# TensorE's unread products in a clustered-attention and softplus-FFN kernel: counts from a rule against counts from a table

## The chip, the cores and the metric

The kernel runs on one core of a Trainium2 chip. The metric is the device time of one execution in microseconds (us); the time shown is the median of several runs, and a profiled execution gives the trace.

## The reference

Inputs are float32 q, k, v of shape (4, 8, 768, 64), centroids (8, 16, 64) and two FFN matrices, 512 x 2048 and 2048 x 512. Every query and key row is assigned to the nearest of 16 normalized centroids of its head; a query attends only to keys of its own cluster. The heads are then joined, and a two-layer network with softplus follows.

```
q_assign = np.argmax(np.einsum('bhsd,hcd->bhsc', q_n, c_n), axis=-1)
k_assign = np.argmax(np.einsum('bhsd,hcd->bhsc', k_n, c_n), axis=-1)
mask = q_assign[:, :, :, None] == k_assign[:, :, None, :]
scores = np.where(mask, scale * np.matmul(q, k.transpose(0, 1, 3, 2)), -1e9)
attn = np.exp(scores - np.max(scores, axis=-1, keepdims=True))
attn = attn / (np.sum(attn, axis=-1, keepdims=True) + 1e-09)
x = np.matmul(attn, v)                    # (B, H, S, D) -> (B*S, H*D)
h = x @ w_in
out = (np.maximum(h, 0.0) + np.log1p(np.exp(-np.abs(h)))) @ w_out
```

## The kernel before

The work is cut into tiles of 128 query rows of one head, 192 in all, taken in eight passes of three row blocks for each of the eight heads. For each tile `scores` (L1101, tile `s`) makes 128 x 768 scores, VectorE takes their negated maximum (L1117, `negm`), ScalarE the exponential (L1126, `p`), and `p` is split into two half-precision parts and transposed: in the first tiles by TensorE (L1143, `pT`), later by a transposing DMA (`pt<-phl`). `attend` (L1239, or L1243 and L1244, into the PSUM tile `mbank`) multiplies by V. Every pass ends in the FFN: `ffn1` (L1331 to L1333, tile `h`), softplus on VectorE, ScalarE and GpSimd, and `ffn2` (L1425 to L1427, tile `o`). The first keys and queries are transposed on TensorE (`turn`, L803, tiles `kT` and `qT`, copied out at L547), compared with the centroids (L822 and L823, tiles `sim_k`, `sim_q`) and masked by a chain of small VectorE operations (L835 to L846, L908); `clusters` counts the clusters in use (L927 on TensorE, L942 on VectorE, `al`).

The order of all instructions is written out: `SEQUENCE` is a list of the numbers of the chains of work, and `Order.run` issues the next operation of the chain that each entry names. `Order` keeps a modelled clock for each engine beside it. The order of entries is the order in the program, engine by engine.

Between these operations TensorE is given products that nobody reads: 128 columns of `ones`, cut to 120, times an identity (L521). `warm` decides on them, before each TensorE operation, from the modelled idle time ahead of it. Where `mbank` is not yet in use they go into its last 120 columns (`idle`), and else into a free one of the three banks of `ps_u` (tile `fill`):

```
gap = end - max(begin, ready)
if gap > (150 if begin < 30000 else WARM_FROM):
    out = idle if spot == 9 else ps_u.tile([P, 512], F32, tag=f"u{spot}", name="fill")[:, :WARM]
    for _ in range(int(gap * (0.95 if begin < 2500 else 0.75 if begin < 30000 else WARM_SHARE) / (100 if begin < 2500 else 52))):
        nc.tensor.matmul(out, eye, ones[:, :WARM], start=True, stop=True)
```

Of the kernel before, what the change touches and what calls it, by code (L numbers as in the profile page):

```python
# [9 lines left out]
F32 = mybir.dt.float32  # L10
# [27 lines left out]
FIRST = 3  # L38
PAIR = 425
WARM = 120  # L40
WARM_FROM = 600
WARM_SHARE = 0.65
FLIP = 180.0
SLACK = 0
BIAS = 500
# [60 lines left out]
]  # L106
SEQUENCE = [
# [166 lines left out]
class Order:  # L274
# [9 lines left out]
    def __init__(self):  # L284
        self.free = {"PE": 1800.0, "DVE": 2500.0, "ACT": 2000.0, "POOL": 2700.0, "SP": 1000.0}
        self.ev, self.blocked, self.active = {}, {}, {}
        self.dma = 0.0
        self.loads = 0
        self.shared = {"DVE": [], "POOL": []}
        self.rings = {}  # L290
        self.cur, self.seq = None, 0
        self.warm = None
        self.mb = [0.0, 0.0]
        self.ranks = iter(RANKS)
        self.mread = 0.0
        self.claims, self.line, self.given = 0, [], {}
        self.held = dict.fromkeys(CAPS, 0)
        self.idle = [("bank", i, 0) for i in range(3)]
        self.ev.update(dict.fromkeys(self.idle, 0.0))
# [104 lines left out]
        return t  # L404

    def run(self):
        for code in SEQUENCE:
            which, seq = divmod(code, 1000)
            ch = self.active.pop(seq)
            _, eng, ns, emit, opt = ch["op"]  # L410
            if isinstance(eng, tuple):
                eng, ns, emit = eng[which], ns[which], emit[which]
            start = self.start(ch, eng, ns)
            if eng == "PE" and self.warm:
                self.warm(self.free["PE"], start)
            self.free[eng] = start + ns - self.PIPE[eng]
            end = start + ns + self.LAT[eng]
            if "flip" in opt:
                self.dma = max(self.dma, start + 900) + opt["flip"]
                self.free[eng] = max(start + ns, self.dma - 1600)  # L420
                end = max(self.dma, self.free[eng]) + 650
            elif "load" in opt:
                self.dma = max(self.dma, start + 900) + opt["load"] + (self.loads == 2) * 1200
                self.loads += 1
                end = max(self.dma, start + ns) + 1350
            if "mb" in opt:
                self.mb[opt["mb"]] = max(self.mb[opt["mb"]], end)
            emit()
            ch["now"] = end
            self.pump(ch)  # L430
        assert not self.blocked and not self.active
# [3 lines left out]
def tile_cluster_attention__then__softplus_ffn(  # L435
# [10 lines left out]
    nc = tc.nc  # L446
# [4 lines left out]
    P = 128  # L451
# [13 lines left out]
            name=nc.get_next_instruction_name(),  # L465
# [10 lines left out]
    ps_u = ctx.enter_context(tc.tile_pool(name="ps_u", bufs=1, space=bass.MemoryType.PSUM))  # L476
# [6 lines left out]
    for c in range(NCL):  # L483
        nc.vector.memset(tab[:, :, c : c + 1], float(NCL - c))

    eye = cpool.tile([P, P], F16, name="eye")
    nc.gpsimd.memset(eye, 0.0)
    nc.gpsimd.affine_select(
        out=eye, in_=eye, compare_op=ALU.not_equal, fill=1.0, base=0, pattern=[[-1, P]], channel_multiplier=1
# [4 lines left out]
    ones = cpool.tile([P, P], F16, name="ones")  # L494
# [13 lines left out]
    od = Order()  # L508
# [2 lines left out]
    mbank = ps_m.tile([P, 512], F32, name="mbank")  # L511
    idle = mbank[:, 512 - WARM :]

    def warm(begin, end):

        ready, spot = min([(od.ev[b], b[1]) for b in od.idle] + [(od.mread, 9)])
        gap = end - max(begin, ready)
        if gap > (150 if begin < 30000 else WARM_FROM):
            out = idle if spot == 9 else ps_u.tile([P, 512], F32, tag=f"u{spot}", name="fill")[:, :WARM]
            for _ in range(int(gap * (0.95 if begin < 2500 else 0.75 if begin < 30000 else WARM_SHARE) / (100 if begin < 2500 else 52))):  # L520
                nc.tensor.matmul(out, eye, ones[:, :WARM], start=True, stop=True)  # L521

    od.warm = warm

# [687 lines left out]
    def attend(t: int):  # L1212
# [6 lines left out]
        if t:  # L1219
            yield wait("at", t - 1)  # L1220
        pt, ptk = pts.pop(t)
        od.mread = math.inf
        t0 = t - t % (2 * nt)
        if whole(t):
            if t == t0:
# [248 lines left out]
    first, begin = {}, []  # L1474
# [13 lines left out]
    for t in range(len(tiles)):  # L1488
        od.spawn(scores(t), t)
        od.spawn(attend(t), t + LAG)  # L1490
# [45 lines left out]
```

## Time and profile before

| what | value |
| --- | --- |
| median of 3 runs | 822.16 us (822.07 to 824.63) |
| profiled execution, its own time | 822.05 us |
| span of its trace | 820.3 us |
| TensorE (PE) busy | 804.5 us, 98% of the span |
| VectorE (DVE), ScalarE (ACT), GpSimd (POOL) busy | 656.3, 563.4 and 543.9 us |
| products at L521 | 269: 187 up to 28.2 us, 82 between 102.4 and 586.6 us |

The time of a run is the span and the little that lies around it. TensorE takes its instructions in order, so a product at L521 holds up whatever stands behind it if that is ready, and costs nothing if it is not. A matmul's row gives the time until its result is out, which reaches into the next one's; the distance between two starts is what one costs in a stream. "Idle before" stands in square brackets, with the work that ended it.

### The profile page before, as it was taken

Reading aid. Unit: us, or ns where it says so; the run is one execution under the profiler, and the core shown is the slowest. Engines: PE = TensorE matmul, PEld = TensorE weight load, DVE = VectorE, ACT = ScalarE, POOL = GpSimd, SP = SyncE. Lnnn points to the kernel's source line nnn. Section 1 sums busy time; section 2 is a strip of 40 time slices with the busy share of each in tenths; the row PEclk is TensorE's granted clock in tenths of the full one; section 3 lists DMA queues with packets and bytes.
Section 4 is the critical chain, followed back from the end, with each engine's and each line's share of the span. In section 5 each row is a group of like instructions: output and inputs, shape, how many; then the busy total and the mean of one; then the engine's idle time right before and its main releaser. Section 6 shows DMA issues by size and latency. Waiting matters only on the chain.

```text
span 820.3 us, 17681 instructions
## 1 busy us (share of the span) xinstructions
PE 804.5 (98%) x6914; PEld 514.2 (63%) x6914; DVE 656.3 (80%) x1124; ACT 563.4 (69%) x1084; POOL 543.9 (66%) x421
## 2 busy tenths in 40 slices
PE   8999999999999999999999999999999999999998
PEld 8888876555666666566666666565666565655554
DVE  7999999998898888888998878969877888743222
ACT  6998899987677767774866867576666656644441
POOL 5856486848877879876477777776876874523340
PEclk9999999999999999999999999999999999999999
DMA  9254999999999999999988988999888885730001
GB/s 334 97 164 142 219 204 237 209 203 212 180 180 193 187 206 182 219 187 173 183 178 172 166 197 180 197 182 196 159 161 151 152 161 110 130 59 13 26 1 40
DMA packets 386228, 134.16 MB, mean 164 GB/s; under 512 B 362464, under 2 KB 379104, under 8 KB 386144
## 3 DMA queue, kind: packets, MB, share of 16 engines
q1 hardware_dynamic: 386144, 133.03, 78.2%
q8 instruction: 54, 0.88, 0.4%
q14 instruction: 30, 0.25, 0.1%
HBM read 35.68 MB, written 6.29 MB: 51 GB/s over the span
## 4 chain that ended last, share of the span: by engine, by line
PE 75%; DMA 7%; DVE 6%; ACT 6%; POOL 3%; issue 3%; SPq 0%; DVEq 0%; ACTq 0%; POOLq 0%
PE s L1101 11%; PE o L1427 8%; PE o L1425 8%; PE o L1426 8%; PE h L1331 8%; PE h L1333 8%; PE h L1332 8%; PE mbank L1243 5%; DMA pt<-phl 4%; PE mbank L1244 3%; PE mbank L1239 2%; POOL phl L556 1%; ACT p L1126 1%; DVE negm L1117 1%; DMA rawk<-in_k_dram 1%
## 5 line engine op out<-in xcount | busy, mean ns | idle before, releaser
L1126 ACT ACTIVATE p<-s,negm 128x768 f32<-128x768 f32 x190 | 170.9, 900 | 77.5 <-DVE negm L1117 55.8
L1117 DVE TENSOR_REDUCE negm<-s 128x1 f32<-128x768 f32 x192 | 181.2, 949 | 25.4 <-PE s L1101 24.6
L556 POOL TENSOR_TENSOR phl<-p,phl 128x768 f16<-128x768 f32 x98 | 171.4, 1754 | 39.1 <-ACT phl L574 26.2
L1331 PE MATMUL h<-xT,wi 128*128 128x384 f16 x512 | 166.9, 326 | 0.6 <-DVE fg L1380 0.3
L1333 PE MATMUL h<-xT,wi 128*128 128x384 f16 x512 | 166.9, 326 | 0.0
L1332 PE MATMUL h<-xT,wi 128*128 128x384 f16 x512 | 166.9, 326 | 0.0
L1101 PE MATMUL s<-kt,qt 128*128 128x384 f16 x768 | 156.3, 326 | 4.6 <-ACT p L1126 2.4
L1425 PE MATMUL o<-wo,gh 128*128 128x512 f16 (+2 forms) x392 | 146.6, 375 | 0.6 <-DVE ot L1458 0.6
L1427 PE MATMUL o<-wo,gh 128*128 128x512 f16 (+2 forms) x392 | 146.5, 375 | 0.3 <-DVE gh L556 0.3
L1426 PE MATMUL o<-wo,gh 128*128 128x512 f16 (+2 forms) x392 | 146.5, 375 | 0.0
L1243 PE MATMUL mbank<-vb,pt 128*128 128x128 f16 x1008 | 107.6, 220 | 0.5 <-DMA pt<-phl 0.4
L556 POOL TENSOR_TENSOR gh<-fg,gh 128x768 f16<-128x768 f32 x47 | 80.2, 1707 | 36.4 <-ACT gh L574 17.5
L1244 PE MATMUL mbank<-vb,pt 128*128 128x64 f16 x1008 | 103.2, 193 | 0.0
L1101 PEld LDWEIGHTS <-qt 128*128 128x128 f16 x768 | 71.0, 98 | 48.8 <-issue 4.4
L1386 POOL TENSOR_TENSOR fg<-fg,fa 128x384 f32<-128x384 f32 x53 | 58.5, 1105 | 63.6 <-ACT fa L1378 61.9
L1243 PEld LDWEIGHTS <-pt 128*128 128x128 f16 x1008 | 89.6, 98 | 14.2 <-DMA pt<-phl 3.0
L1244 PEld LDWEIGHTS <-pt 128*128 128x128 f16 x1008 | 87.7, 98 | 10.9
L1362 ACT ACTIVATE fa<-h 128x384 f32<-128x384 f32 x84 | 41.0, 488 | 68.9 <-PE h L1333 51.4
L574 ACT CAST phl<-p 128x768 f16<-128x768 f32 x87 | 71.4, 827 | 17.4 <-DMA pt<-phl 14.4
L556 DVE TENSOR_TENSOR phl<-p,phl 128x768 f16<-128x768 f32 x64 | 71.0, 1113 | 4.2 <-POOL phl L574 2.4
L1377 ACT ACTIVATE fa<-fa 128x384 f32<-128x384 f32 x128 | 66.5, 522 | 9.6 <-DVE fa L1358 8.9
L1332 PEld LDWEIGHTS <-wi 128*128 128x128 f16 x512 | 50.1, 98 | 34.9 <-issue 1.8
(193 smaller groups left out, 1429.8 us busy)
## 6 DMA issues: line engine op xcount, KB each, us to landing
wo<-in_moe_w_in_dram SPq DMA_DIRECT2D x8, 1024.0 KB, 7.7
rawk<-in_k_dram SPq DMA_DIRECT2D x16, 384.0 KB, 3.9
rawq<-in_q_dram SPq DMA_DIRECT2D x16, 384.0 KB, 4.2
rawv<-in_v_dram SPq DMA_DIRECT2D x16, 384.0 KB, 4.0
wo<-in_moe_w_out_dram SPq DMA_DIRECT2D x6, 1024.0 KB, 5.7
out_dram<-ot SPq DMA_DIRECT2D x23, 256.0 KB, 2.6
pt<-phl SPq DMA_TRANSPOSE x82, 5.7
wo<-in_moe_w_out_dram SPq DMA_DIRECT2D x2, 512.0 KB, 4.0
```

The source lines that it names most:

```text
L556: [lambda e=e: e.tensor_tensor(dst, a, b, ALU.subtract) for e in (nc.gpsimd, nc.vector)],
L1101: nc.tensor.matmul(st[:, j, :SH], qt[:, s, i], kt[:, s, NT // 2 * j : NT // 2 * (j + 1)], start=(s == 0), stop=(s == 1),)
L1117: yield op("DVE", 950, lambda: nc.vector.tensor_reduce(negm, st[:, :, :SH], AX.XY, ALU.max, negate=True))
L1126: yield op("ACT", 980, lambda: nc.scalar.activation(ex, st[:, :, :SH], AF.Exp, bias=negm, accum_out=total))
L1243: nc.tensor.matmul(av, pt[:, 0, c], vb[:, c, : 2 * D], start=(c == 0), stop=False)
L1244: nc.tensor.matmul(av[:, D:], pt[:, 1, c], vb[:, c, D : 2 * D], start=False, stop=(c == NT - 1))
L1331: nc.tensor.matmul(hp, w[0], x[0], start=(c == 0), stop=False)
L1332: nc.tensor.matmul(hp, w[0], x[1], start=False, stop=False)
L1333: nc.tensor.matmul(hp, w[1], x[0], start=False, stop=(c == NP - 1))
L1425: nc.tensor.matmul(out_, g[0], wo[:, f, 0, 0, side], start=(f == f0), stop=False)
L1426: nc.tensor.matmul(out_, g[0], wo[:, f, 0, 1, side], start=False, stop=False)
L1427: nc.tensor.matmul(out_, g[1], wo[:, f, 0, 0, side], start=False, stop=(f == f0 + NF // 2 - 1))
```

## The change

The rule is replaced by a table, `FILLS`, from the place in `SEQUENCE` to a number of products. All of them go into `mbank`'s last columns. The table holds 14 places, all before entry 178 of the list, and 148 products. The constants `WARM_FROM` and `WARM_SHARE` and the variable `mread` go.

```
+FILLS = {
+    16: 42, 22: 15, 31: 14, 46: 9, 67: 13, 90: 8, 108: 10, 112: 6, 119: 3, 125: 7, 133: 2, 150: 7, 170: 6, 177: 6,
+}
...
-        for code in SEQUENCE:
+        for at, code in enumerate(SEQUENCE):
...
-            if eng == "PE" and self.warm:
-                self.warm(self.free["PE"], start)
+            if at in FILLS:
+                self.warm(FILLS[at])
...
-    def warm(begin, end):
-
-        ready, spot = min([(od.ev[b], b[1]) for b in od.idle] + [(od.mread, 9)])
-        gap = end - max(begin, ready)
-        if gap > (150 if begin < 30000 else WARM_FROM):
-            out = idle if spot == 9 else ps_u.tile([P, 512], F32, tag=f"u{spot}", name="fill")[:, :WARM]
-            for _ in range(int(gap * (0.95 if begin < 2500 else 0.75 if begin < 30000 else WARM_SHARE) / (100 if begin < 2500 else 52))):
-                nc.tensor.matmul(out, eye, ones[:, :WARM], start=True, stop=True)
+    def warm(count):
+        for _ in range(count):
+            nc.tensor.matmul(idle, eye, ones[:, :WARM], start=True, stop=True)
```

Everything else of the program stands in the same order on all five engines. By the start of each group in the trace of before, the counts are:

| start, us | 1.84 | 6.96 | 8.25 | 9.49 | 12.38 | 14.26 | 16.49 | 18.39 | 19.66 | 21.49 | 21.87 | 23.57 | 25.57 | 28.01 |
| --- | --- | --- | --- | --- | --- | --- | --- | --- | --- | --- | --- | --- | --- | --- |
| before | 42 | 15 | 14 | 11 | 18 | 24 | 12 | 12 | 6 | 4 | 7 | 2 | 15 | 5 |
| change | 42 | 15 | 14 | 9 | 13 | 0 | 8 | 10 | 6 | 3 | 7 | 2 | 7 | 6 |

The 3 of the tenth column stand ahead of the six `kT` products at 21.16 us, where the 4 stood behind them, and six more stand behind the `pT` products at 29.29 us. The groups at 102.36 us (11), 104.62 us (13), 110.97 us (23), 299.88 us (25) and 586.16 us (10) have no counterpart.

On TensorE, after the comparison of the second pair of key heads with the centroids (`sim_k`, L822 and L823) and ahead of the next transposes of masked keys (`kT`), about 14 us into the run, before:

```order
L822 MATMUL sim_k_411<-cents,kt_234 128x16
L823 LDWEIGHTS kt_234
L823 MATMUL sim_k_411<-cents,kt_234 128x16
L521 LDWEIGHTS eye
L521 MATMUL mbank<-ones,eye 128x120
...
L803 LDWEIGHTS kn_0_131
L803 MATMUL kT_0_0_443<-eye,kn_0_131 128x128
```

The same place in the change, where the lines of the program stand 4 or 5 lower and buffers have other numbers:

```order
L818 MATMUL sim_k_403<-cents,kt_233 128x16
L819 LDWEIGHTS kt_233
L819 MATMUL sim_k_403<-cents,kt_233 128x16
L799 LDWEIGHTS kn_0_131
L799 MATMUL kT_0_0_435<-eye,kn_0_131 128x128
```

The 24 products between the two are gone, and the transposes follow the comparison directly.

On TensorE, about 300 us into the run, between the scores of one tile (`s`) and the product of another tile's transposed weights with V (`mbank<-vb,pt`), before:

```order
L1101 LDWEIGHTS qt_3_4067
L1101 MATMUL s_3_4565<-kt_2524,qt_3_4067 128x384
L521 LDWEIGHTS eye
L521 MATMUL fill<-ones,eye 128x120
...
L1243 LDWEIGHTS pt_4_4507
L1243 MATMUL mbank<-vb_102,pt_4_4507 128x128
```

The same place in the change:

```order
L1097 LDWEIGHTS qt_3_3977
L1097 MATMUL s_3_4475<-kt_2434,qt_3_3977 128x384
L1238 LDWEIGHTS pt_4_4417
L1238 MATMUL mbank<-vb_102,pt_4_4417 128x128
```

The 25 products are gone; the product with V follows the scores.

## Rows read from the trace of the kernel before

**Rows 1.** The page: busy us (share of the span), instructions; slices; instruction queue.

```profile
PE 804.5 (98%) x6914; PEld 514.2 (63%) x6914; DVE 656.3 (80%) x1124; ACT 563.4 (69%) x1084; POOL 543.9 (66%) x421
...
PEclk9999999999999999999999999999999999999999
...
q8 instruction: 54, 0.88, 0.4%
```

**Rows 2.** Chain that ended last, 7 to 31 us: start us, us, what.

```profile
7.12 0.79 PE mbank L521 x15
...
14.41 1.28 PE mbank L521 x24
...
19.80 0.33 PE mbank L521 x6
...
20.19 0.84 issue
...
29.69 0.38 ACT qt L547
```

**Rows 3.** TensorE in order of time, 1 to 31 us: start us, us, work [idle before].

```profile
1.84 4.16 PE L521 MATMUL fill<-ones,eye 128*128 128x120 f16 x42 [1.84 <-DVE down L659]
...
14.26 1.42 PE L521 MATMUL mbank<-ones,eye 128*128 128x120 f16 x24
15.52 0.50 PE L803 MATMUL kT<-eye,kn 128*128 128x128 f16 x6
...
21.03 0.28 PE L803 MATMUL qT<-eye,n 128*128 128x128 f16 x2 [0.84 <-issue]
...
30.11 0.33 PE L803 MATMUL qT<-eye,qn 128*128 128x128 f16 x3 [0.32 <-ACT qt L547]
```

**Rows 4.** VectorE in order of time, 13 to 25 us.

```profile
13.69 0.20 DVE L908 TENSOR_SCALAR kn<-kn 128x192 f16<-128x192 f16 x1
...
16.34 0.19 DVE L942 TENSOR_SCALAR al<-sim_k 128x32 f16<-128x32 f32 x1 [0.43 <-PE sim_k L927]
16.69 0.56 DVE L547 COPY kt<-kT 128x768 f16<-128x768 f16 x1 [0.16 <-PE kT L803]
...
23.77 1.82 DVE L1117 TENSOR_REDUCE negm<-s 128x1 f32<-128x768 f32 x2
```

**Rows 5.** ScalarE in order of time, 15 to 31 us.

```profile
21.36 0.48 ACT L547 COPY qt<-qT 128x384 f16<-128x384 f16 x1 [0.93 <-PE qT L803]
...
24.90 0.95 ACT L1126 ACTIVATE p<-s,negm 128x768 f32<-128x768 f32 x1
```

**Rows 6.** Chain that ended last, pieces at 300, 515 and 586 us.

```profile
300.05 1.31 PE fill L521 x25
...
514.77 7.27 DMA pt<-phl
...
586.32 0.53 PE fill L521 x10
```

**Rows 7.** Busy us of PE, PEld, DVE, ACT, POOL (instructions); clock, DMA share, GB/s.

```profile
300.00:400.00 100.00, 100.00 (x874) 61.64 (x872) 85.91 (x157) 67.56 (x133) 75.86 (x57) 1.00 0.98 192
```

**Rows 8.** TensorE in order of time, 87 to 113 us.

```profile
87.48 0.50 PE L1101 MATMUL s<-kt,qt 128*128 128x384 f16 x2 [1.40 <-DMA qt<-n]
...
103.46 0.81 PE L1101 MATMUL s<-kt,qt 128*128 128x384 f16 x4 [0.37 <-ACT p L1126]
...
104.62 0.85 PE L521 MATMUL fill<-ones,eye 128*128 128x120 f16 x13
...
110.97 1.37 PE L521 MATMUL fill<-ones,eye 128*128 128x120 f16 x23
112.95 0.81 PE L1101 MATMUL s<-kt,qt 128*128 128x384 f16 x4 [0.61 <-DVE phl L1189]
```

**Rows 9.** Chain that ended last, 103 to 107 us.

```profile
103.46 3.73 DMA rawk<-in_k_dram
```

**Rows 10.** VectorE in order of time, 498 us.

```profile
498.68 0.77 DVE L830 TENSOR_REDUCE sim_k<-sim_k 128x128 f32<-128x256 f32 x2 [0.63 <-PE sim_k L820]
```

More of the change, by code (lines that the diff above doesn't have):

```diff
@@ L40 @@
 WARM = 120
-WARM_FROM = 600
-WARM_SHARE = 0.65
 FLIP = 180.0
@@ L294, in __init__ @@
         self.ranks = iter(RANKS)
-        self.mread = 0.0
         self.claims, self.line, self.given = 0, [], {}
@@ L1221, in attend @@
         pt, ptk = pts.pop(t)
-        od.mread = math.inf
         t0 = t - t % (2 * nt)
```

## The prediction

> **What bounds the kernel now.** I read the page first: TensorE is busy 98% of the span, no other engine over 80%, and its granted clock stands at full level in all 40 slices [rows 1]. So the question is which of the 121 products that go (269 against 148) stand on the chain that ends last. The chain of waits tells that. Between 7 and 21 us it runs on TensorE, and eight groups of unread products are pieces of it, from the first, of 15 in 0.79 us, over the longest, of 24 in 1.28 us, to the last, of 6 in 0.33 us; after them come 0.84 us in which TensorE waited for nothing that the profile shows, and from 21.36 to 30.07 us the chain runs on ScalarE [rows 2, 5]. TensorE's own order of time shows how the 24 hold up work: they start at 14.26, the next transposes at 15.52 us, without a mark of waiting [rows 3]. VectorE's order of time shows that engine nearly full there, with two marked waits for TensorE, 0.43 and 0.16 us [rows 4]. ScalarE has no marked wait between the one that ends at 21.36 us and 30 us [rows 5]. Much later the chain holds two more groups whole: 25 products, 1.31 us, at 300 us and 10 products, 0.53 us, at 586 us [rows 6]. From 300 to 400 us TensorE has no idle time at all [rows 7].
>
> **The change, part by part.** One product costs 52.5 ns in a stream at the full clock: 1.26 us from 14.26 to 15.52 us for 24 of them [rows 3].
>
> *The first 42.* They stay. They take 4.16 us, 99 ns each, and TensorE then waits for VectorE before it transposes; that they now write `mbank` instead of a bank of `ps_u` changes nothing before VectorE is done. Nothing is gained or lost [rows 3].
>
> *The other early groups.* Up to the 0.84 us stall the groups lose 2, 5, 24, 4 and 2 products, 37 in all: 37 x 52.5 ns = 1.94 us of the chain, the upper bound of what TensorE can gain in them. With the stall, should that vanish, it is 2.78 us. The lower bound is 0. How much of it reaches 30 us is decided by what is late next, and that is VectorE. The masked keys that the 24 held up had been finished at 13.89 us [rows 4], so the transposes can follow at 14.26 us, and the L927 products and transposes that VectorE waits for at 16.34 and 16.69 us come up to 1.26 us sooner. VectorE can use only its idle time, 0.43 + 0.16 = 0.59 us; waits of under 0.15 us that the view leaves unmarked add a little. Its `negm` of the first scores at 23.77 us takes about half of 1.82 us, to 24.68 us, and the exponential on ScalarE starts at 24.90 us [rows 4, 5], so there are another 0.22 us before VectorE holds ScalarE up. That makes 0.81 us. ScalarE itself has 0.93 us to give at 21.36 us, where it waits for TensorE [rows 5]; the smaller counts, and so I take **0.8 us**. From there ScalarE works without a break until TensorE, idle for 0.32 us, gets its query transposes at 30.11 us [rows 2, 3], and the 0.8 us pass to TensorE whole. The edits from 21 to 30 us (4 products that become 3 and stand one step earlier, 15 that become 7, 5 that become 6, and 6 new ones) lie beside this run of ScalarE and cost nothing; the new ones need 6 x 52.5 ns = 0.32 us, which is the idle time ahead of 30.11 us.
>
> *The groups at 102 to 111 us.* They have 47 products, 47 x 52.5 ns = 2.47 us, at most. But behind the first TensorE still waited 0.37 us for ScalarE and behind the last 0.61 us for VectorE [rows 8], and the chain runs past all three through a load of keys and the engines behind it [rows 9]. Their cover is that load; the second group lies between the two waits and its gain ends in the 0.61 us. I take 0, with an upper bound of 0.68 us for the 13 of the second group.
>
> *The two late groups.* At 300 us TensorE goes straight from the scores to the product with V, and saves 25 x 52.5 ns = **1.31 us**; at 586 us 10 x 52.5 ns = **0.52 us**. Both stand on the chain with their full length [rows 6]. The bounds are 0 and these. I take the full ones, since no row marks a wait behind either. Whether the first lasts is seen at 498.68 us, where the chain leaves TensorE for VectorE and goes on to a transposing DMA that lands 7.27 us after its piece begins [rows 6, 10]: VectorE waited there 0.63 us for TensorE. Its earlier work, which waits for TensorE too, should move along; if it doesn't, 0.63 us remain of 1.31.
>
> *Waits.* Without `fill` tiles the next products into those banks need not wait for the unread ones, and no wait is added. No queue but TensorE's changes.
>
> Sum: 0.8 + 1.31 + 0.52 = 2.63 us off the profiled execution's own 822.05 us, 819.4 us. The median is 0.11 us above that execution, so I forecast **819.5 us**, 0.32% faster. A measurement of this kernel can tell about 0.3%, 2.47 us, from no change, so the forecast lies just beyond that bound.
>
> [...] TensorE's instructions come in 54 packets of 0.88 MB together, about 16 KB each [rows 1], and the idle 0.84 us at 21.03 us had no releaser [rows 3]. [...]
>
> **The rivals.**
>
> *A, TensorE sets the early pace.* If VectorE's small operations run quicker once they are bunched, the early gain goes to its bound, 2.78 us, and the time to 822.16 - 2.78 - 1.83 = 817.5 us. For it speaks that the chain lies on TensorE until 21 us; against it that VectorE has so little idle time [rows 4].
>
> *B, the stall moves.* 37 products with their weight loads are 74 instructions. If the stall belongs to a place in the instruction stream, it now comes 74 instructions later in the program, near the first scores (L1101), for which the `negm` at 23.77 us waits. It would take back 0.8 us: 822.16 - 1.83 = 820.3 us. Against it: TensorE gets there with 1.94 - 0.8 = 1.1 us in hand, and only a stall longer than the 0.84 us of before would use that up.
>
> *C, the late gain is given back.* Transposing DMAs and GpSimd are the chain at 500 to 522 us [rows 6]. If these keep their times, only 0.8 us or little more remains: 821.4 us. Against it: in 300 to 400 us VectorE, ScalarE and GpSimd are busy 86, 68 and 76 us of 100 [rows 7] and can follow.
>
> [...]
>
> **How the numbers follow.** Forecast 0.62, A 0.09, B 0.13, C 0.08, D 0.08. The forecast has a spread of some 0.4 us of its own, the small waits and the 0.81 against 0.93 us; about two thirds of it, 0.41, lie beyond 2.47 us. Faster: 0.41 + 0.09 = 0.5. Within 0.3%: 0.21 + 0.13 + 0.08 = 0.42. Slower: 0.08. The range leaves out A and D, together 0.17: it runs from 818.3 us, where the early part gains 2 us, to 821.5 us, just over C.
>
> **What would show it.** VectorE's marks at 16.34 and 16.69 us gone; the exponential at 24.90 us some 0.8 us earlier, and the query transposes at 30.11 us too; the product with V behind the 25 about 2.1 us earlier, the scores behind the 10 about 2.6 us earlier; the clock full throughout. At 112.95 us the move should still be 0.8 us. It is wrong if the move at 31 us is below 0.3 or above 1.3 us, if it shrinks between 301 and 523 us, or if the granted clock drops anywhere.

## The result, and the profile after

The change takes 830.4 us (median of 4 runs, 830.05 to 832.7) against 822.26 us before (4 runs beside it): a ratio of 1.0098, 95% interval 1.0072 to 1.0124. That is 8.1 us slower where 2.6 us faster was forecast. The profiled execution took 830.09 us, its span is 828.3 us, 8.0 us more than before.

The page of the change, in the parts of [rows 1], then the shares of the chain that ended last by engine, and the groups of the scores and of the product with V:

```profile
PE 802.0 (97%) x6793; PEld 508.0 (61%) x6793; DVE 662.5 (80%) x1124; ACT 564.3 (68%) x1084; POOL 542.9 (66%) x421
...
PEclk9999999999999999999999999999999999999999
...
q8 instruction: 53, 0.87, 0.4%
...
PE 58%; DVE 16%; DMA 12%; ACT 6%; POOL 4%; issue 3%; DVEq 0%; ACTq 0%; POOLq 0%
...
L1097 PE MATMUL s<-kt,qt 128*128 128x384 f16 x768 | 156.4, 326 | 8.2 <-ACT p L1122 6.0
...
L1238 PE MATMUL mbank<-vb,pt 128*128 128x128 f16 x1008 | 107.6, 220 | 5.4 <-DMA pt<-phl 3.9
```

The last three of these on the page of before:

```profile
PE 75%; DMA 7%; DVE 6%; ACT 6%; POOL 3%; issue 3%; SPq 0%; DVEq 0%; ACTq 0%; POOLq 0%
...
L1101 PE MATMUL s<-kt,qt 128*128 128x384 f16 x768 | 156.3, 326 | 4.6 <-ACT p L1126 2.4
...
L1243 PE MATMUL mbank<-vb,pt 128*128 128x128 f16 x1008 | 107.6, 220 | 0.5 <-DMA pt<-phl 0.4
```

The clock is full in every slice, the work that is read is the same and TensorE's busy time is 2.5 us less; but the chain has left TensorE for 17% of the span, and new idle time stands ahead of the scores (3.6 us more) and of the product with V (4.9 us more). The second has a new releaser, the transposing DMA `pt<-phl`.

Where the time was lost is told by the start of the same ScalarE instruction in both traces, change less before (us):

| at, us | 28 | 76 | 130 | 210 | 292 | 311 | 400 | 500 | 582 | 645 | 800 |
| --- | --- | --- | --- | --- | --- | --- | --- | --- | --- | --- | --- |
| change | -1.09 | -1.06 | -0.26 | -0.69 | 0.27 | 0.67 | 3.88 | 6.76 | 8.42 | 8.17 | 8.04 |

The early gain is there, and larger than forecast. (Four kernels further down have the change's program unaltered up to 240 us; at 28 us their moves are -1.23, -1.18, -0.98 and -0.25 us, so that a single trace is good to some half a microsecond.) The loss comes between 230 and 580 us, in many steps of up to 1.3 us, in a stretch from which the change only takes work away. The windows of TensorE there (columns as in [rows 7], whose row stands between the two), before:

```profile
200.00:300.00 100.00, 99.94 (x861) 61.78 (x860) 84.77 (x143) 71.96 (x138) 80.12 (x60) 1.00 0.99 188
...
400.00:500.00 100.00, 100.00 (x847) 61.39 (x845) 85.33 (x131) 71.33 (x145) 74.00 (x58) 1.00 0.88 176
```

and after:

```profile
200.00:300.00 100.00, 98.51 (x849) 60.67 (x848) 79.88 (x137) 70.56 (x135) 78.23 (x59) 1.00 1.00 190
300.00:400.00 100.00, 97.24 (x827) 58.77 (x825) 88.39 (x158) 65.51 (x129) 72.01 (x55) 1.00 1.01 184
400.00:500.00 100.00, 97.91 (x810) 59.36 (x808) 87.62 (x129) 68.64 (x139) 71.17 (x54) 1.00 0.88 174
```

TensorE, almost without a gap before, now waits 1.5 to 2.8 us in each 100. Gaps over 150 ns between 112 and 640 us add up to 2.7 us before and 11.9 us after. One of the first such waits, in TensorE's order of time after the change:

```profile
260.62 0.81 PE L1097 MATMUL s<-kt,qt 128*128 128x384 f16 x4
262.23 0.23 PE L1238 MATMUL mbank<-vb,pt 128*128 128x128 f16 x1 [0.81 <-DMA pt<-phl]
```

The transpose for which it waits, as the view of the tile `pt` gives it: issued at 255.0 us, who waited for it, and the time from issue to landing.

```profile
L594 SPq DMA_TRANSPOSE pt<-phl x1: 3658/3658/3658, 255.0 to 255.0; - x1
...
  PEld L1238: 1.2, 1
  PE mbank L1238: 0.8, 1
  ACT phl L570: 0.8, 1
  DVE phl L570: 0.6, 1
...
DMA to landing us min/median/max: 7.2/7.2/7.2
```

The same transpose before:

```profile
L598 SPq DMA_TRANSPOSE pt<-phl x1: 3614/3614/3614, 255.9 to 255.9; - x1
...
DMA to landing us min/median/max: 5.5/5.5/5.5
```

It is the same transfer, issued by SyncE in the same time, and it lands 1.7 us later. What differs is shown by the DMA view. In the change, from 260.0 to 260.4 us, one row is not data:

```profile
q8 instruction: 1, 0.02, 14.6%
```

One packet of TensorE's instructions came at 260.15 us, 5.15 us after the issue and just ahead of the landing. Before, no such packet lies between this transpose's issue and its landing; its packets came at 248.0 and 265.0 us. The change takes 172 TensorE instructions (86 products and their weight loads) out of the stream by then, and q8 has about one packet for every 256 of them: 54 packets with 2 x 6914 before, 53 with 2 x 6793 here, and 55 with 2 x 7042 in a kernel further down, while the other engines' instructions are the same. So the packets come at other places of the work.

Counted over the 82 `pt` transposes from 30 to 800 us in each trace: those with no instruction packet of any engine in them take 5.57 us before and 5.58 us after (medians). 16 before and 16 after have a packet of TensorE 4.6 to 5.6 us after their issue; these take 6.82 and 7.05 us in the mean. In 11 before and 15 after, more than 3 us pass from the end of the issuing to the landing, where about 1.9 us are usual; all of the 11 and 14 of the 15 have such a packet. As many are met before as after, and from 150 to 640 us all of them together take 396.8 and 397.5 us. But they are others, and TensorE waits for some of the new ones.

### The profile page after: what moved, and what is told of

Same layout as the page of the kernel before. It is cut to its first block, busy times and chain, and to the rows that moved or that the text cites. A ratio compares the mean times of both kernels' runs of the same rounds, so it can differ in the third digit from the quotient of the medians.

```text
span 828.3 us, 17439 instructions
## 1 busy us (share of the span) xinstructions
PE 802.0 (97%) x6793; PEld 508.0 (61%) x6793; DVE 662.5 (80%) x1124; ACT 564.3 (68%) x1084; POOL 542.9 (66%) x421
## 4 chain that ended last, share of the span: by engine, by line
PE 58%; DVE 16%; DMA 12%; ACT 6%; POOL 4%; issue 3%; DVEq 0%; ACTq 0%; POOLq 0%
DMA pt<-phl 9%; PE s L1097 8%; PE o L1422 7%; PE o L1420 7%; PE o L1421 7%; PE h L1326 6%; PE h L1327 6%; PE h L1328 6%; PE mbank L1238 4%; DVE negm L1113 4%; DMA wo<-in_moe_w_out_dram 2%; PE mbank L1239 2%; PE mbank L1234 2%; POOL phl L552 2%; ACT p L1122 1%
## 5 line engine op out<-in xcount | busy, mean ns | idle before, releaser
L552 DVE TENSOR_TENSOR phl<-p,phl 128x768 f16<-128x768 f32 x64 | 74.7, 1170 | 6.1 <-ACT phl L570 3.8
L570 POOL CAST phl<-p 128x768 f16<-128x768 f32 x54 | 49.7, 923 | 35.3 <-ACT p L1122 21.8
```

The source lines that it names most:

```text
L552: [lambda e=e: e.tensor_tensor(dst, a, b, ALU.subtract) for e in (nc.gpsimd, nc.vector)],
```

## The experiments

Theory F: the places of TensorE's instruction packets decide. A packet that falls into a transposing DMA makes it late; where TensorE, or an engine that feeds it, needs that one soon, the time is lost. Theory G: what counts is the missing work of the unread products themselves, above all of the five groups from 102 us on, which kept TensorE's pace. All ratios are to the kernel before, run on the same chip.

### The places given back without the work, and moved without it

To the change, one-column products were added where each group lost some, so that from 30 us on every TensorE instruction has its old place in the stream:

```
+TINY = {46: 2, 67: 5, 76: 24, 90: 4, 108: 2, 121: 1, 150: 1, 533: 11, 553: 13, 580: 23, 1494: 25, 2837: 10}
...
+            if at in TINY:
+                self.warm(TINY[at], 1)
```

> The change, but each unread product that it drops is replaced, at its place, by a product of one column (39 early ones, 82 late ones), so that every other instruction of TensorE stands at the same place in its instruction stream as before. Theory F (fetch): a 16 KB packet of TensorE's instructions that meets the end of a transposing DMA makes it take 7.2 us where it takes 5.5 us, and the change moves these meetings onto transposes that TensorE waits for; then the loss goes, and 819.5 to 822 us come out. Theory G (work): the unread products' own work between 102 and 586 us is needed; then it stays at 829 to 831 us.

Measured: 822.87 us (10 runs), ratio 0.9992 (0.9976 to 1.0008), span 820.2 us. The time is 0.9 us over the range expected, but the 8 us are gone, with products of one column, 25 ns each. The early gain went with them: at 28 us the move is -0.17 us only, and TensorE stands 1.49 us without a releaser at the products that had the 0.84 us before [rows 3]. So this kernel alone can't tell the packets from the early shift in time; the kernels below can. The converse: the kernel before, with 42 of its early products cut into two of 60 columns.

```
-                nc.tensor.matmul(out, eye, ones[:, :WARM], start=True, stop=True)
+                parts = 2 if 2500 < begin < 30000 and halves[0] > 0 else 1
+                halves[0] -= parts - 1
+                for _ in range(parts):
+                    nc.tensor.matmul(out[:, : WARM // parts], eye, ones[:, : WARM // parts], start=True, stop=True)
```

> The kernel before, with 42 of its early unread products cut in two of 60 columns each: the same work, but 84 TensorE instructions more, which puts the blocks of 256 where they stand in the change between 111 and 300 us. F: slower, 825 to 832 us, with more waits of TensorE for transposing DMAs after 111 us. G: 822 to 823 us.

Measured: 830.55 us (4 runs), ratio 1.0089 (1.0074 to 1.0104). The same columns in 84 more instructions before 30 us cost as much as the change. 1.6 us of it are lost at once, by 30 us; the rest comes step by step, 2.5 us in all at 210, 4.5 at 292 and 7.3 us at 500 us. 84 more and 172 fewer differ by 256, one packet, so from 113 to 300 us the packets stand at the same places of the work as in the change, and the same waits are there. The transpose that was issued at 255.0 us in the change, here:

```profile
L603 SPq DMA_TRANSPOSE pt<-phl x1: 3677/3677/3677, 259.4 to 259.4; - x1
...
  PE mbank L1248: 0.6, 1
...
DMA to landing us min/median/max: 7.1/7.1/7.1
```

Its packet came 5.06 us after the issue, against 5.15 in the change. The products with V that stood at 121.8, 166.6, 262.0 and 291.1 us before wait for `pt` 0.36, 0.19, 0.81 and 0.68 us in the change, 0.38, 0.32, 0.65 and 0.77 us here, and without a marked wait before.

### Each half of the change alone

The five late groups put back into the change (by a table like the one above, with their full width), and the kernel before without them (`if begin < 30000 and gap > 150:`).

> The early part of the change alone: the five late groups are back (11, 13, 23, 25 and 10 products of 120 columns). TensorE's instructions stand 78 places earlier all the way. F: the early gain of 1.1 us at 31 us comes, and what the moved blocks cost is open: 820 to 832 us, and long transposes stand where a packet of instructions meets their end. G: 821 us.

> The late part of the change alone: the early groups as before, the five late ones gone. TensorE's instructions stand 94 places earlier from 113 us, 144 from 300 us and 164 from 587 us. F: open, 820 to 832 us, again told by the long transposes. G: about 831 us, since the work that is gone is the same as in the change.

Measured: 829.2 us, ratio 1.0083 (1.0063 to 1.0104), and 827.49 us, ratio 1.0053 (1.0038 to 1.0068). Either half alone is slower than before, and together they are hardly slower than one. Costs of work would add up; a new draw of places need not. G, by which the first would have taken 821 and the second 831 us, falls.

### The change with its packets moved

In the change, 17, 43, 64 or 86 of the early products are cut in two, with the same edit in `warm(count)`. That gives back 34, 86, 128 or 172 instructions; 172 are as many as the change has lost at 113 us.

> The change with 17 of its early products cut in two of 60 columns: the same columns, 34 more TensorE instructions from 22 us on, so that each 16 KB packet of TensorE's instructions comes 34 instructions earlier in the work. Theory F (packets meet other transposing DMAs): another draw, by the kernels so far 827 to 831 us, 822 if few transposes that TensorE waits for are met; PE idle from 112 to 640 us 3 to 12 us, and the time follows it. Theory G (the products that went did something themselves): 830.4 as the change, within 1 us.

> The change with 43 early products cut in two: 86 more TensorE instructions from about 40 us on, half of the way back to the places of before between 113 and 300 us. Theory F: the time differs from that of the change by more than 1 us in most such kernels; between 820 and 832, and TensorE's idle time from 112 to 640 us differs by as much. Theory G: 830.4, within 1 us.

> The change with 64 early products cut in two: 128 more TensorE instructions, half a packet. Theory F: packets come half-way between those of the change; 820 to 832, as TensorE's idle time from 112 to 640 us tells. Theory G: 830.4, within 1 us.

> The change with 86 early products cut in two: 172 more TensorE instructions, as many as the change takes away up to 113 us, so that from there to 300 us every packet stands where it stood before; from 300 us 50 and from 587 us 70 instructions short of it. Theory F: no step of the time against the kernel before from 113 to 300 us (the change lost about 1.2 us there from 230 to 310 us), steps after 300 us where other packets are met: 822 to 827 us. Theory G: 830.4, within 1 us, with the change's steps in the same places.

| products cut | 17 | 43 | 64 | 86 |
| --- | --- | --- | --- | --- |
| median, us | 827.07 | 829.22 | 829.74 | 824.51 |
| ratio | 1.0056 | 1.0084 | 1.0084 | 1.0013 |
| 95% interval | 1.0033 to 1.0079 | 1.0056 to 1.0112 | 1.0059 to 1.0108 | 1.0000 to 1.0025 |

The times differ by 5 us with the same columns of work. (64 cut, within 1 us of the change, fits G as well as F; 17 and 86 cut don't fit G.) Places are not the only difference, though: the cutting has its early cost, and in three of the four traces TensorE's granted clock falls, which it doesn't in the change. With 17 cut it is 0.50 for 3.41 us from 62.99 us on, with 43 cut three times (its trace, of an execution of 836.89 us, isn't used further). With 86 cut it falls behind a long wait (the second line has the columns of [rows 7]):

```profile
113.98 0.82 PE L1102 MATMUL s<-kt,qt 128*128 128x384 f16 x4 [2.50 <-DVE phl L1190]
...
114.64:118.05 3.41, 3.41 (x37) 2.74 (x36) 2.71 (x4) 3.35 (x7) 1.30 (x2) 0.50 0.76 144
```

That costs the last kernel 1.6 us between 113 and 130 us, a step that the expectation didn't have. Behind it, it is the sharpest: its move against the kernel before is 2.64 us at 130 us, 2.67 at 210 and 2.67 at 292 us, without a step and at the full clock, where the change lost 0.5 us and the kernels with 17 and 64 cut lost 3.1 and 2.7 us, at the full clock too. At 300 us it falls to 1.36: the 25 products that are gone there give their full 1.31 us when nothing else happens. The window of TensorE in this kernel:

```profile
200.00:300.00 100.00, 99.93 (x848) 61.28 (x847) 83.78 (x141) 71.94 (x137) 80.61 (x61) 1.00 1.00 188
```

### A whole packet, and places paid for in waits

In the first kernel, 128 products of the kernel before are cut, 256 instructions more. In the other two, the change gets one-column products only where TensorE waits anyway, at 102 and 111 us: `TINY = {533: 30, 580: 56, 1494: 25, 2837: 10}`, and without the last two.

> The kernel before with 128 of its early products cut in two of 60 columns: 256 more TensorE instructions by 30 us, one whole packet, so that the packets after that come at the same places of the work as before (one more of them in all). Theory F: early cost 1 to 2 us as with the 42 cut (+1.6 us at 76 us), and no step after 130 us: 823 to 825.5. If more instructions of TensorE cost time by their number and not by place: more than with 84 of them, above 830.5.

> The change, with 86 one-column products (172 TensorE instructions) put where TensorE waits anyway, at 102 and 111 us, and 25 and 10 of them where the last two groups stood: from 113 us on every packet of TensorE's instructions stands where it stood before, and up to 30 us nothing is given back of the early gain. Theory F: about 0.5 us of the early gain is left at 113 us, as in the change; no step from 113 to 300 us; span 819.5 to 821, time about 0.5 us below the kernel before. Theory G: as the change, 829 to 831.

> The same with none of the 25 and 10 at 300 and 587 us: packets stand as before from 113 to 300 us, 50 instructions early from there, 70 from 587 us, as in the kernel with 86 products cut in two. Theory F: no step up to 300 us, then as that kernel from 300 us to the end, which lost nothing there (+2.67 us at 292 us, +2.54 at 800): span 819 to 821. Theory G: 829 to 831.

The whole packet took 828.73 us, ratio 1.0066 (1.005 to 1.0082), and not the 823 to 825.5 us expected. But the loss is early: the move is 5.73 us at 28 us already, 5.49 at 292, 5.42 at 500 and 6.17 us at 800 us. With three times the extra instructions of the 42 cut, it lost 0.4 us after 28 us where those lost 6.1 us. So place decides, as F says, and the early price was mis-sized. What it consists of stands in TensorE's order of time and in a window (columns as in [rows 7]):

```profile
14.12 0.61 PE L526 MATMUL mbank<-ones,eye 128*128 128x60 f16 x16 [0.78 <-issue]
...
20.58 1.21 PE L526 MATMUL mbank<-ones,eye 128*128 128x60 f16 x21 [2.57 <-issue]
...
19.91:26.74 6.83, 6.16 (x116) 6.16 (x116) 1.99 (x9) 1.93 (x3) 1.37 (x3) 0.50 0.62 254
```

With 128 pairs of such short products TensorE stood for 0.78 and then 2.57 us with no releaser, 2.5 us more than before, and from 19.91 us, within the second of these waits, its granted clock was 0.50 for 6.83 us. TensorE was busy for 6.16 us of that; as an estimate, half of it, some 3 us, is the price of the clock. The two make up nearly all of the 5.73 us.

The two others took 822.74 us, ratio 0.9995 (0.9981 to 1.0008), and 821.42 us, ratio 0.9983 (0.9967 to 0.9999). The second is the one version that beats both kernels: by 1.1% the change, and by 0.17% the kernel before, which is only just told from no difference, for one of fifteen kernels tried. The expectation of no step from 113 us on held from 130 us only: between 113 and 130 us the moves rise by 0.6 and 1.6 us. The packet at 115.5 and 115.8 us meets the transpose of 110 us 5.0 and 5.5 us after its issue, it takes 7.4 and 7.65 us, and TensorE waits; in the second kernel:

```profile
118.02 0.23 PE L1247 MATMUL mbank<-vb,pt 128*128 128x128 f16 x1 [0.82 <-DMA pt<-phl]
```

Taken together, the moves tell packets from time. From 130 to 292 us they rise by 0.45 us or less in all five kernels that have the packets of before there, though these stand from 0.7 us ahead to 5.7 us behind at 28 us. In all eleven others, the change among them, they rise by 0.5 to 4.8 us.

### One transpose at a time

The last question was whether the single transpose is long because of the packet. Products of the FFN's first half were issued as 128 and 256 columns, 11 of 12 in a row (`cuts = ((0, 1), (1, 3))` over the three row blocks), 22 instructions more.

> The change with one row of products of the second half (12 products of 384 columns at 245 to 247 us, h of pass 2, f 2) issued as 128 and 256 columns in 11 of the 12: the same columns in the same order, 22 more TensorE instructions from 246 us on, nothing else. Theory F: all is as in the change up to 246 us; every packet of TensorE's instructions after that comes some 1.3 us earlier in the work (22 instructions at about 17 a us), so the transpose issued at 255.0 us, hit 5.15 us after its issue, is met at about 3.9 us, takes 5.5 to 6.0 instead of 7.18 us, and the wait of 0.81 us at 262 us goes; the same for those of 284.9 and 300.7 us (7.21, 7.24). After that other transposes are met; the time is another draw, 822 to 830 us. A rival H, in which the long transposes come from what else the queues move and the packet is only there by chance: 255.0 us still takes 7.2 us, the waits stay, 830 us.

Measured: 828.93 us, ratio 1.0069 (1.0045 to 1.0093). The expectation named the wrong place: the row that was cut (pass 2, f 2) ran at 296.9 us, 52 us later, so that nothing was tested for 255.0 and 284.9 us, and both took 7.2 and 7.1 us again. For 300.7 us it was a test, and F as put there missed: 7.07 us with the packet at 5.00 us after the issue. That a packet due 1.3 us earlier (an estimate: 22 instructions, at the 17 a us of TensorE's window above) still came 5 us after the issue suggests, though no view shows it, that it is held: over the 82 transposes of either trace, before and change, no packet of TensorE came 3.3 to 4.6 us after an issue, and 16 came 4.6 to 5.6 us after one. It is not without exceptions: in the fifteen other traces together 18 came 3.3 to 4.6 us after an issue, and 254 came 4.6 to 5.6 us after one. The next three cut rows at the right place.

> As the run before it, at the right place: the row of products at 244.8 to 247.3 us (h of pass 1, f 10) issued as 128 and 256 columns in 11 of its 12 products, 22 more TensorE instructions from 247 us on. Theory F, refined (a packet that is asked for while a pt transpose moves is held until some 5.1 us after that transpose's issue, and both come late): in the change the packet of 260.2 us came 71 instructions after the earliest place in its block, 4.2 us, so it was asked for at 256.0 us, 1.0 us after the issue of the transpose of 255.0; 22 instructions earlier is 254.7, at the edge, so 255.0 may go either way; the one of 300.7 us (asked for at 302.3, now 301.0) is still met: 7.1 us.

> The same in two rows (pass 1, f 9 and 10, 240 to 247 us): 44 more instructions. Theory F, refined: asked for 2.6 us earlier, at 253.4, 282.7 and 299.7 us, before the transposes of 255.0, 284.9 and 300.7 us are issued; all three take 5.4 to 6.2 us instead of 7.18, 7.21 and 7.24, and the waits on pt at 262 (0.81 us) and 292 us (0.68 us) go. Rival H (the packet is there by chance): 7.2 us and the waits stay.

> The same in three rows (pass 1, f 9 to 11, 240 to 251 us): 66 more instructions. Theory F, refined: asked for 3.9 us earlier, at 252.1, 281.4 and 298.4 us; all three transposes take 5.4 to 6.2 us, the waits at 262 and 292 us go. Rival H: they stay.

| kernel | profiled execution, us | transpose of 255 us: took (packet after issue) | of 285 us | of 300 us |
| --- | --- | --- | --- | --- |
| change | 830.09 | 7.18 (5.15) | 7.21 (5.20) | 7.24 (5.13) |
| 22 more | 829.91 | 5.98 (0.79) | 7.12 (5.11) | 7.10 (5.03) |
| 44 more | 826.49 | 5.73 (0.95) | 5.45 (0.25) | 6.99 (4.81) |
| 66 more | 824.46 | 5.57 (none) | 5.54 (0.26) | 5.47 (0.33) |

The view of `pt` in the third kernel, for the transposes issued at 255.8 and then at 266.4 us:

```profile
L594 SPq DMA_TRANSPOSE pt<-phl x1: 3910/3910/3910, 255.8 to 255.8; - x1
...
DMA to landing us min/median/max: 5.6/5.6/5.6
...
L594 SPq DMA_TRANSPOSE pt<-phl x1: 3525/3525/3525, 266.4 to 266.4; - x1
...
  POOL phl L570: 1.9, 1
  ACT phl L570: 0.7, 1
  PEld L1238: 0.2, 1
...
DMA to landing us min/median/max: 7.4/7.4/7.4
```

The three are single executions, so their times say less than their transposes. With 66 instructions all three came as F said, and the waits at 262 and 292 us are gone. With 44 two did, and the third missed. With 22, the packet of the first fell from 5.15 to 0.79 us after the issue, by 4.4 us for 22 instructions, which fits a packet that is held or isn't. Rival H falls. The packet that left the transpose of 255 us met the one of 266 us, which took 7.4 us, and no matmul of TensorE has a marked wait for that one. So what counts is which transposes are met, more than how many: from 150 to 640 us those of the kernel with 66 take 407.1 us in all, 9.6 us more than in the change, and its profiled execution is 5.6 us faster.

## Why the prediction was wrong

*The early part* was right in its mechanism. VectorE's marks at 16.34 and 16.69 us [rows 4] are gone, its `negm` of the first scores starts at 22.82 us, and the exponential of 24.90 us [rows 5] and the transposes of 30.11 us [rows 3] come 1.10 and 1.09 us sooner. VectorE's order of time after the change:

```profile
16.03 0.55 DVE L543 COPY kt<-kT 128x768 f16<-128x768 f16 x1
...
22.82 1.81 DVE L1113 TENSOR_REDUCE negm<-s 128x1 f32<-128x768 f32 x2
```

ScalarE's, with a wait for VectorE ahead of the exponential:

```profile
23.80 0.90 ACT L1122 ACTIVATE p<-s,negm 128x768 f32<-128x768 f32 x1 [0.77 <-DVE negm L1113]
```

TensorE's, at the query transposes and at the scores that stood at 112.95 us:

```profile
29.02 0.33 PE L799 MATMUL qT<-eye,qn 128*128 128x128 f16 x3
...
112.42 0.81 PE L1097 MATMUL s<-kt,qt 128*128 128x384 f16 x4 [1.64 <-DVE phl L1185]
```

The term was 0.8 and measured 1.09 us, inside the bounds given. Half of it was lost by 112 us: 0.53 us are left at the scores of 112.95 us, where 0.8 were to be. In the four kernels with the same program up to 240 us, 0.70, 0.51 and 0.20 us are left there, and one is 0.17 us behind.

*The groups at 102 to 111 us* cost and brought nothing there, as forecast: where they stood, TensorE now waits 1.64 us for VectorE [rows 8].

*The late groups.* 1.31 and 0.52 us were right as the price of the work: with 86 products cut the move falls by 1.31 us at 300 us. "I take the full ones, since no row marks a wait behind either" failed in the change itself, where behind the scores of 300.35 us TensorE waits 0.70 us for VectorE's `x`; the move fell by about 0.45 us there, and by 0.53 us at 587 us.

```profile
300.35 0.81 PE L1097 MATMUL s<-kt,qt 128*128 128x384 f16 x4
301.86 0.22 PE L1238 MATMUL mbank<-vb,pt 128*128 128x128 f16 x1 [0.70 <-DVE x L1256]
```

*The step that failed* is "No queue but TensorE's changes", and with it the sum, which held only work and marked waits. TensorE's stream of instructions is itself a transfer, 53 or 54 packets long [rows 1]. Taking 172 instructions out of it by 113 us, 242 in all, moves every later packet. I had asked of these packets only whether TensorE waits for one of them (rival B), and not what they do to the transfers beside them. A row that shows it stood in front of me: the piece of 7.27 us at 514.77 us [rows 6] is a transpose of a kind that usually takes 5.57 us, and a packet came 5.27 us after its issue. I took it as the transfer's own time.

The price: 8.7 us were lost between the scores of 112.42 us and 645 us. Behind these scores (the 1.64 us ahead of them took the place of products that went) TensorE's gaps up to 640 us grew by 8.2 us; less the 1.83 us of work that went, that is 6.4 of the 8.7 us. The rest stands in TensorE's busy time, whose rows for the same products are 2.4 us longer in all between 250 and 500 us. Of the 8.2 us, the waits on `pt` are 3.5 us. Most others are waits on ScalarE's `p` and on VectorE; the engines that write `phl` wait for late transposes too, as the view of `pt` shows (0.8 us for ScalarE at 255.0 us), but that all of them come from this was not shown one by one.

*The rivals.* A fails: 1.09 us, not 2.78. B fails as to the time: up to 31 us the change has no wait without a releaser. But its premise holds, the stall belongs to a place in the stream. In seven of the seventeen traces TensorE waits over 0.4 us with no releaser up to 32 us, each time at its 224th or its 351st product, 127 products or about 256 instructions apart, and goes on 2.3 to 2.5 us after a packet's start. The change reaches the 351st at 22.31 us, 3.84 us after the packet, and need not wait. C fails in its cause: a step of some 0.8 us at 520 us is there with the late products in place too (the kernel with a whole packet more, 5.42 us at 500 and 6.22 at 582 us). D, a slower kernel by a fall of TensorE's clock when unread products go, rested on no run: no row of before shows such a fall, and in its place the change showed a granted clock of 1.00 in all four executions, through the 1.64 us of idling as well. That alone would not do, since the slices are full over the first 42 products too, which ran at 99 ns [rows 1, 3]; but the scores and the products with V take 326 and 220 ns in the mean, before and after. In two test kernels the granted clock did fall to 0.50, though: with 86 products cut behind a wait of 2.50 us, with 128 within one of 2.57 us. The chance of slower, 0.08, rested on D alone; the true mechanism was in none of the cases, so the range could not hold it.

Of TensorE's own waits in the change none lacks a releaser up to 31 us. In other traces some do: 0.84 us before, 1.49 us with the places given back and 2.57 us with 128 products cut. In the change the price of the packets lies, as far as it was shown, in the transposes that they meet.

## What to carry to other kernels

When an edit adds or removes instructions on an engine, ask what else is moved: here TensorE's instructions came in 53 to 55 packets on a DMA queue, one per about 256 of them; where one met a transpose that TensorE needed soon, TensorE waited (0.81 us at 262 us), and with the same columns of work the time went from 824.51 to 829.74 us with the places and the price of the cutting. Of the 11 kernels here whose packets stood at other places than before between 113 and 300 us, none came under 824.4 us. An edit's own worth can be told from this lottery by keeping the count: put one-column products (25 ns each) where the engine waits anyway, or cut products in two, compare, and look at the granted clock of each trace before the times are set side by side. Where one transfer in a long row of equal ones takes 7.2 us instead of 5.6, look for what else moved at its end before taking it as its time.

## What the hardware showed that was not expected

- A `pt` transpose that has a packet of TensorE's instructions (about 16 KB) 4.6 to 5.6 us after its issue takes 6.8 to 7.2 us in the mean of the kernels, where 5.6 us are usual. Why it is so much, for a packet that small (the one at 260.15 us took 0.93 us), was not found.
- Packets of TensorE seldom came 3.3 to 4.6 us after the issue of such a transpose, and often 4.6 to 5.6, as if they were held until it is nearly done: 22 instructions, about 1.3 us of the work, moved one from 5.15 to 0.79 us after the issue, and left others at 5.0 to 5.1. Of 304 packets that came 3.3 to 5.6 us after an issue, in all seventeen traces, 18 came before 4.6 us.
- TensorE stood without a releaser at its 224th or its 351st product in each of the seven traces where it did for over 0.4 us up to 32 us: 0.84 us before [rows 3], and 2.57 us in the kernel with 128 products cut.
- The granted clock fell to 0.50 in four of the test kernels, with 17, 43, 86 and 128 products cut, for 3.41 or 6.83 us at a time (0.997, 0.991, 0.997 and 0.995 in the mean of their traces), and in the traces of neither the kernel before nor the change.
- The number of TensorE's instructions ahead of 30 us alone, with the same columns, changed the time by about 1% (84 more: 830.55 us).
